# Attention scores of two heads in four contract over 68 partitions instead of 128, and two clears go

## The chip, the cores and the metric

The kernel runs on one core of a Trainium2 chip. The metric is the device time of one execution in microseconds, the median of the runs. The core's engines are PE (matrix multiply; PEld is its weight load), DVE (VectorE), ACT (ScalarE), POOL (GpSimd) and SP, which issues transfers. Each works through its own instructions in order and waits on semaphores for the others.

## What is computed

Eight batches of eight heads of causal attention over 576 positions with 64 features, with a bias from a running sum, and behind it a feed-forward block over all 4608 tokens:

```python
scores = q @ k.T / 8                       # per head, 576 x 576
cum    = cumsum(maximum(s, 0))
scores = where(causal, -1e9, scores + minimum(-(cum[i] - cum[j]), 0))
attn   = softmax(scores) @ v               # 64 heads
x      = attn, heads side by side          # 4608 x 512
g, val = x @ w_gate, x @ w_val             # 512 -> 1536
out    = (silu(g) * val) @ w_out           # 1536 -> 512
```

## The kernel before

The 64 heads are worked off in 16 half-batches of four heads. The query and key rows of a half-batch stand, transposed, in two tiles `KQ[i][0]` and `KQ[i][1]` (i is the half-batch modulo 2), each of 128 partitions, with an index for key side (0) and query side (1) and the positions of two heads, 2 x 576 columns, and 64 columns of padding behind them. In `KQ[i][0]` the 64 features are in partitions 0 to 63, in `KQ[i][1]` in partitions 64 to 127. The other 64 partitions carry the bias: four of them ("aug" rows: partitions 64 to 67 of the first tile, 0 to 3 of the second) hold the running sum, split into a high and a low bf16 part, against constant rows, so that one matmul gives the product of query and key and the bias in one sum. The remaining 60 are zero, so that the contraction over all 128 partitions is right. Heads 0 and 1 of a half-batch are in the first tile, heads 2 and 3 in the second.

`score_piece` (L352) makes the scores of one head, in four chunks of 512, 512, 512 and 64 columns, each in one PSUM bank; in all nine matmuls a head at L373, with 128, 128, 128, 128 / 448, 64 / 320, 192 / 64 columns. ACT takes the exponential (L383). For the first batch a mask matmul (L367) comes first in the chunks on the diagonal; for later batches POOL clears above the diagonal afterwards. `av_piece` (L410) multiplies with the values, DVE divides (L427). `gate_value` (L643) and the down projections (L700, L749) are the feed-forward block; they are mixed with the attention of later batches in an order that is written out by hand and by a list of costs, which fixes each engine's order of work.

The beginning is written out too. The clears of the 60 zero partitions stand there: DVE clears half of the columns of the first tile of half-batch 0 (L222), ACT both second tiles (L230), POOL the first tile of half-batch 1 (L234); `pads` (L226) clears the padding columns. DVE then makes the running sum (L240, L241), splits it into `HL` (L244 to L246) and copies transposed queries and keys out of PSUM (L330). For the very first head the aug rows are not brought by a transfer (`aug`, L188): PE picks them out of `HL` (L914), and ACT (L925) and DVE (L929) write all of partitions 64 to 127 of its columns. POOL issues the loads of half-batch 1 (L145) behind its clears, casts (L270), and issues the loads of v (L162).

Of the kernel before, what the change touches and what calls it, by code (L numbers as in the profile page):

```python
# [19 lines left out]
def kernel(  # L20
# [11 lines left out]
    nc = tc.nc  # L32
    PSUM = bass.MemoryType.PSUM

    B, H, S, D = q.shape
# [7 lines left out]
    NR = HB // 2  # L43
# [20 lines left out]
    def pt_col(tj, bi):  # L64
# [26 lines left out]
    KQ = [  # L91
        [const.tile([128, 2, NR * S + 64], BF16, name=f"kq{e}{i}") for e in range(2)]
        for i in range(2)
    ]
# [19 lines left out]
    with tc.manual_schedule():  # L114
# [10 lines left out]
        def take():  # L125
            b = min(bank, key=lambda x: released[x])
            assert released[b] < OPEN
            released[b] = OPEN
            return b

        def give(b):
            clock[0] += 1
            released[b] = clock[0]

        def view(b, w):
            return bank[b][:, 0:w]
# [42 lines left out]
        def aug_rows(i, r):  # L179
            r0 = 64 * (1 - r)  # L180
            return KQ[i][r][r0 : r0 + 64, :, :].bitcast(FP32)
# [37 lines left out]
        nc.vector.tensor_add(r_k[up], ident[up, 64:65], ident[up, 65:66])  # L219
        nc.vector.tensor_add(r_q[up], ident[up, 66:67], ident[up, 67:68])  # L220
        nc.vector.tensor_scalar_mul(r_m[up], r_q[up], -1.0)
        nc.vector.memset(aug_rows(0, 0)[:, :, S // 2 :], 0.0)  # L222

        def pads(i):
            for r in range(2):
                nc.gpsimd.memset(KQ[i][r][64 * r : 64 * r + 64, :, NR * S :], 0.0)  # L226

        for i in range(2):
            rows = aug_rows(i, 1)
# [1 line left out]
                rows.rearrange("p a n -> p (a n)"),  # L231
                one_s[0:64, 0:1].to_broadcast([64, NR * S + 64]), 0.0,
            )
        nc.gpsimd.memset(aug_rows(1, 0), 0.0)  # L234
        pads(0)
        pads(1)
        for nm in ("k", "q"):
            load_one(1, nm, eng=nc.gpsimd)
# [113 lines left out]
        def score_piece(bh, ci):  # L352
            hb, hh = divmod(bh, HB)
            masked = bh < H
            if ci == 0:
                pts[bh] = PTP[0].tile(
                    [128, PTW], BF16, tag="pt", bufs=PTP["bufs"], name="pt"
                )
            pt = pts[bh]
            r, e = divmod(hh, 2)  # L360
            T = KQ[hb % 2][r]
            bs = take()
            n = sum(hi - lo for _, lo, hi in CHUNKS[ci])
            sc = view(bs, n)
            masked_here = masked and ci in (0, 3)
            if masked_here:
                nc.tensor.matmul(  # L367
                    sc, ident, lower[:, 0:n], start=True, stop=False, skip_group_check=True
                )
            o = 0  # L370
            for (tj, lo, hi) in CHUNKS[ci]:
                w = hi - lo
                nc.tensor.matmul(  # L373
                    sc[:, o : o + w],
                    T[:, 1, e * S + 128 * tj : e * S + 128 * (tj + 1)],
                    T[:, 0, e * S + lo : e * S + hi],
                    start=not masked_here,
                    stop=True,
                    skip_group_check=masked_here,
                )  # L380
                o += w
            c0 = CHUNK_PT[ci]
            nc.scalar.activation(pt[:, c0 : c0 + n], sc, AF.Exp, scale=0.125)  # L383
            give(bs)
            if masked:
                return
            if ci == 0:
                nc.gpsimd.affine_select(  # L388
                    pt[:, 1088:1600], pt[:, 1088:1600], pattern=[[0, 4], [1, 128]],
                    compare_op=ALU.is_ge, fill=zreg, base=0, channel_multiplier=-1,  # L390
                )
            if ci == 3:
                nc.gpsimd.affine_select(
                    pt[:, 512:576], pt[:, 512:576], pattern=[[1, 64]],
                    compare_op=ALU.is_ge, fill=zreg, base=0, channel_multiplier=-1,
                )
# [164 lines left out]
        def attn_items():  # L561
            for kk in range(H, BH + 2):
                h, step = divmod(kk, HB)
                if kk < BH:
                    if step == 0:
                        do_later(NR * 2)
                    if step == 1 and 3 < h + 1 < NPE:
                        cast_one(h + 1, "k", nc.gpsimd)
                        cast_one(h + 1, "q", nc.gpsimd)
                    if step == 2 and 3 < h + 1 < NPE:  # L570
                        aug(h + 1, GP4)
                    for ci in range(4):
                        score_piece(kk, ci)
                        side(h, step, ci)
                        side_v(h, step, ci)
                        yield kk + 0.1 + ci / 8
                        if (step, ci) in PREP_AT.get(h, ()):
                            prep_one(
                                h + 1, PREP_AT[h][step, ci],
                                (nc.scalar, nc.vector)[ci // 2] if h == 2 else None,  # L580
                            )
                            yield kk + 0.1 + ci / 8
# [357 lines left out]
        def scores(h):  # L940
            for ci in range(4):
                score_piece(h, ci)
# [22 lines left out]
        picked_row(0)  # L965
        row_half("k", 1)
        score_piece(0, 0)
        score_piece(0, 1)
        row_half("q", 1)
# [151 lines left out]
```

## Time and profile before

| | |
|---|---|
| median of 3 runs | 374.26 us (373.94 to 375.38) |
| the profiled execution's own time | 373.92 us |
| its span, first to last instruction | 372.0 us |
| mean granted clock of PE | 0.998 |
| PE busy | 363.2 us |
| score matmuls L373, 576 in all: mean with 128 / 64 / 448 / 320 / 192 columns | 219 / 193 / 352 / 299 / 246 ns |
| their weight loads, mean | 98 ns |
| DVE clear L222, POOL clear L234 | 0.59 us, 1.11 us |

A matmul's row has the active rows and columns of the array ahead of its shape: 128\*128 is all of it, 64\*128 are 64 partitions contracted. Matmuls are pipelined, so the duration of one is a latency that overlaps the next; the throughput is the distance between starts. A time such as "8.44 0.89" is the start and the length in microseconds.

### The profile page before, as it was taken

Reading aid. Unit: us, or ns where it says so; the run is one execution under the profiler, and the core shown is the slowest. Engines: PE = TensorE matmul, PEld = TensorE weight load, DVE = VectorE, ACT = ScalarE, POOL = GpSimd, SP = SyncE. Lnnn points to the kernel's source line nnn. Section 1 sums busy time; section 2 is a strip of 40 time slices with the busy share of each in tenths; the row PEclk is TensorE's granted clock in tenths of the full one; section 3 lists DMA queues with packets and bytes.
Section 4 is the critical chain, followed back from the end, with each engine's and each line's share of the span. In section 5 each row is a group of like instructions: output and inputs, shape, how many; then the busy total and the mean of one; then the engine's idle time right before and its main releaser. Section 6 shows DMA issues by size and latency. Waiting matters only on the chain.

```text
span 372.0 us, 8786 instructions
## 1 busy us (share of the span) xinstructions
PE 363.2 (98%) x3288; PEld 230.3 (62%) x3288; DVE 291.1 (78%) x585; ACT 239.9 (65%) x470; POOL 212.4 (57%) x325
## 2 busy tenths in 40 slices
PE   7899999999999999999999999999999999999996
PEld 6684556655555557855685558655865585476465
DVE  8978776377985899589967897699868867975984
ACT  8877776778886967688757875786565523323321
POOL 8983556955266547594749464955675516315320
PEclk9999999999999999999999999999999999999999
DMA  7999999799879996996789484994142113002003
GB/s 238 220 254 259 215 272 257 239 299 227 252 172 307 199 268 181 162 285 217 214 179 263 160 185 157 265 210 114 40 121 62 35 30 118 0 3 86 28 0 113
DMA packets 97133, 64.21 MB, mean 173 GB/s; under 512 B 77228, under 2 KB 82724, under 8 KB 97092
## 3 DMA queue, kind: packets, MB, share of 16 engines
q1 hardware_dynamic: 84964, 41.46, 46.9%
q0 software_dynamic: 12128, 22.21, 22.7%
q8 instruction: 25, 0.41, 0.5%
q14 instruction: 16, 0.13, 0.1%
HBM read 37.90 MB, written 19.86 MB: 155 GB/s over the span
## 4 chain that ended last, share of the span: by engine, by line
PE 83%; DVE 10%; DMA 2%; ACT 2%; issue 2%; POOL 1%; DVEq 0%; ACTq 0%
PE banks L643 43%; PE banks L749 17%; PE banks L373 9%; PE banks L410 7%; PE banks L700 5%; DVE kq L330 3%; DMA pk<-ks 2%; DVE pp L666 2%; DVE ht L677 1%; DVE kq L288 1%; ACT th L664 1%; POOL vt L173 1%; ACT pt L383 1%; PE banks L459 1%; PE banks L301 0%
## 5 line engine op out<-in xcount | busy, mean ns | idle before, releaser
L383 ACT ACTIVATE pt<-banks 128x512 bf16<-128x512 f32 (+1 forms) x256 | 120.4, 511 | 29.8 <-PE banks L373 17.1
L643 PE MATMUL banks<-XT,wg 128*128 128x512 bf16 x432 | 111.4, 379 | 0.4 <-DVE pp L666 0.3
L643 PE MATMUL banks<-XT,wv 128*128 128x512 bf16 x432 | 110.9, 379 | 0.1
L664 ACT ACTIVATE th<-banks 128x512 bf16<-128x512 f32 x108 | 64.7, 599 | 56.3 <-PE banks L643 51.4
L666 DVE SCALAR_TENSOR_TENSOR pp<-th,banks 128x512 bf16<-128x512 bf16 x108 | 73.7, 682 | 18.3 <-ACT th L664 18.0
L677 DVE SCALAR_TENSOR_TENSOR ht<-pp,banks 128x512 bf16<-128x512 bf16 x108 | 74.1, 687 | 10.3
L373 PE MATMUL banks<-kq 128*128 128x128 bf16 (+4 forms) x576 | 76.4, 240 | 0.8 <-DVE kq L330 0.3
L686 POOL TENSOR_TENSOR ht<-ht 128x512 bf16<-128x512 bf16 x35 | 40.4, 1154 | 53.3 <-DVE su L684 53.2
L373 PEld LDWEIGHTS <-kq 128*128 128x128 bf16 x576 | 46.1, 98 | 30.7 <-issue 2.4
L643 PEld LDWEIGHTS <-wv 128*128 128x128 bf16 x432 | 38.4, 98 | 36.2 <-issue 0.2
L643 PEld LDWEIGHTS <-wg 128*128 128x128 bf16 x432 | 38.4, 98 | 34.1 <-issue 0.7
L410 PEld LDWEIGHTS <-pt 128*128 128x128 bf16 x960 | 41.8, 98 | 17.7 <-issue 0.7
L388 POOL TENSOR_SCALAR_AFFINE_SELECT pt<-pt 128x512 bf16<-128x512 bf16 x56 | 36.6, 653 | 25.9 <-ACT pt L383 21.7
L410 PE MATMUL banks<-vt,pt 128*128 128x65 bf16 x960 | 46.8, 194 | 0.5 <-DVE ot L427 0.4
L444 POOL DMA_DIRECT2D xs<-ot x24 | 21.7, 904 | 30.4 <-DVE ot L427 28.0
L749 PEld LDWEIGHTS <-ht 128*128 128x128 bf16 x336 | 31.2, 98 | 4.3
L427 DVE TENSOR_TENSOR ot<-banks,rc 128x320 bf16<-128x320 f32 x64 | 31.5, 492 | 2.2
L188 POOL DMA_DIRECT2D kq<-HL x48 | 29.2, 610 | 0.0
L700 PE MATMUL banks<-wo,ht 128*128 128x512 bf16 x96 | 25.8, 379 | 0.0
L749 PEld LDWEIGHTS <-su 128*128 128x128 bf16 x252 | 23.6, 98 | 3.3
L814 POOL TENSOR_TENSOR ysb<-ysb 128x512 f32<-128x512 f32 x12 | 15.2, 1269 | 15.3 <-DVE ysb L808 15.3
L749 PE MATMUL banks<-WS,ht 128*128 128x256 bf16 x168 | 22.9, 273 | 0.0
(101 smaller groups left out, 377.2 us busy)
## 6 DMA issues: line engine op xcount, KB each, us to landing
out_dram<-ysb POOLq DMA_DIRECT2D x32, 256.0 KB, 4.0
rawv<-in_v_dram SPq DMA_DIRECT2D x28, 256.0 KB
rawk<-in_k_dram SPq DMA_DIRECT2D x12, 576.0 KB
rawq<-in_q_dram SPq DMA_DIRECT2D x12, 576.0 KB
xs<-ot POOLq DMA_DIRECT2D x24, 160.0 KB, 3.7
ks<-ck SPq DMA_DIRECT2D x11, 288.0 KB
qs<-cq SPq DMA_DIRECT2D x11, 288.0 KB
rawk<-in_k_dram POOLq DMA_DIRECT2D x3, 576.0 KB, 6.0
```

Of the source, the lines that this page charges most:

```text
L373: nc.tensor.matmul(sc[:, o : o + w], T[:, 1, e * S + 128 * tj : e * S + 128 * (tj + 1)], T[:, 0, e * S + lo : e * S + hi], start=not maske ...
L383: nc.scalar.activation(pt[:, c0 : c0 + n], sc, AF.Exp, scale=0.125)
L388: nc.gpsimd.affine_select(pt[:, 1088:1600], pt[:, 1088:1600], pattern=[[0, 4], [1, 128]], compare_op=ALU.is_ge, fill=zreg, base=0, channel ...
L410: nc.tensor.matmul(av[:, bi * (D + 1) : (bi + 1) * (D + 1)], pt[:, c0 : c0 + 128], VT[b % 2][:, tj, h, :], start=(tj == 0), stop=(tj == bi),)
L427: nc.vector.tensor_mul(ot[:, :, e * D : (e + 1) * D], av3[:, :, 0:D], rc[:, :, None].to_broadcast([128, NCH, D]),)
L643: nc.tensor.matmul(view(bs, TT), w[:, c, f0 : f0 + 128], xt[:, c, :], start=(c == 0), stop=(c == 3),)
L664: nc.scalar.activation(th, pg, AF.Tanh, scale=0.5)
L666: nc.vector.scalar_tensor_tensor(pp, in0=th, scalar=1.0, in1=pg, op0=ALU.add, op1=ALU.mult)
L677: nc.vector.scalar_tensor_tensor(hp[:, 2 * k2 : 2 * k2 + 2, :].rearrange("p a n -> p (a n)"), in0=pp, scalar=0.5, in1=pv, op0=ALU.mult, op ...
L686: (nc.vector if ft == NFT - 1 else nc.gpsimd).tensor_sub(hp[:, 1:3, :], hp[:, 1:4:2, :], hp[:, 0:3:2, :])
L700: nc.tensor.matmul(view(pys[ts_], DM), hps[ft // 2][:, 2 * (ft % 2) + half, c0 : c0 + 128], WO[j][:, ft % WKO, :], start=(ft == 0), stop=( ...
L749: nc.tensor.matmul(ps, lhs(p), rhs(p), start=(first and p == 0), stop=(last and p == NP - 1), skip_group_check=True,)
```

## The change

The scores of heads 0 and 1 of each half-batch take only partitions 0 to 67 of the first tile, the features and the four aug rows; those of heads 2 and 3 still take all 128. The two clears of zero partitions of the first tiles go, and `pads` clears the padding of the query side alone, for the first tile over all partitions. The order of everything else is as it was.

```diff
-        nc.vector.memset(aug_rows(0, 0)[:, :, S // 2 :], 0.0)
 
         def pads(i):
             for r in range(2):
-                nc.gpsimd.memset(KQ[i][r][64 * r : 64 * r + 64, :, NR * S :], 0.0)
+                nc.gpsimd.memset(KQ[i][r][64 * r :, 1, NR * S :], 0.0)
...
-        nc.gpsimd.memset(aug_rows(1, 0), 0.0)
         pads(0)
         pads(1)
...
             r, e = divmod(hh, 2)
-            T = KQ[hb % 2][r]
+            T = KQ[hb % 2][r][0 : 68 if r == 0 else 128]
             bs = take()
```

## The prediction, made before the changed kernel was built or run

> **What bounds the kernel now.** I read the page first, then the busy time by stretches, the chain of waits of the first 20 us, the timeline of the same stretch, and one line's own view. The page's span and its row of busy time:
>
> ```profile
> span 372.0 us, 8786 instructions
> ...
> PE 363.2 (98%) x3288; PEld 230.3 (62%) x3288; DVE 291.1 (78%) x585; ACT 239.9 (65%) x470; POOL 212.4 (57%) x325
> ```
>
> The busy time by stretches says where the missing 2% lie (stretch, its length, then each engine's busy time):
>
> ```profile
> 0.00:9.30 9.30, 7.05 (x68) 5.58 (x69) 7.93 (x19) 7.74 (x10) 8.28 (x19) 1.00 0.72 238
> 9.30:19.00 9.70, 8.38 (x96) 6.05 (x96) 9.54 (x15) 8.47 (x21) 9.58 (x14) 1.00 1.01 219
> 19.00:100.00 81.00, 79.81 (x840) 48.95 (x836) 59.41 (x116) 63.78 (x125) 47.93 (x81) 1.00 1.05 253
> 100.00:200.00 100.00, 99.60 (x935) 63.50 (x932) 79.92 (x166) 72.86 (x145) 62.97 (x99) 1.00 0.92 219
> 200.00:300.00 100.00, 100.00 (x928) 63.55 (x926) 82.61 (x173) 66.85 (x135) 61.96 (x93) 1.00 0.57 139
> ```
>
> From 19 us on PE hardly ever idles. "Busy" overlaps, so I also took the distance from each matmul's start to the next in the trace and subtracted its columns at 2.4 per ns: from 19 us to the last matmul at 368 us all of that comes to 11.6 us, mostly 2 to 3 ns on each of some 3100 matmuls; real stalls are about 3 us. So after 19 us the time is the number of columns that PE streams, and only two things can move it: the price of a score matmul, and when the dense part begins. What sets that beginning is in the chain of waits (start, length, what):
>
> ```profile
> 3.11 0.59 DVE kq L222
> 3.70 0.03 issue
> 3.73 0.56 DVE s_sb L240
> ...
> 6.97 0.80 DVE HL L246
> 7.77 0.61 DVE kq L330
> 8.38 0.06 issue
> 8.44 0.17 DVE kq L929
> ```
>
> The clear at L222 stands in a DVE line without gaps: prefix sum, split into HL, first copies, row L929. From 9.24 to 19.36 DVE goes on so, 9.54 busy of 9.70 us. The timeline shows who else meets it:
>
> ```profile
> 2.61 1.11 POOL L234 MEMSET kq<- 64x1216 f32 x1
> ...
> 4.85 0.91 POOL L145 DMA_DIRECT2D rawk<-in_k_dram  x1
> ...
> 6.15 0.69 PE L315 MATMUL banks<-ident,cq 128*64 128x128 bf16 x9
> ...
> 6.77 1.15 PE L914 MATMUL banks<-HL,sel 64*128 64x512 bf16 x8
> ...
> 7.86 0.69 PE L315 MATMUL banks<-ident,ck 128*64 128x128 bf16 x9
> 8.00 0.82 ACT L925 ACTIVATE kq<-banks,r_m,r_k 64x576 bf16<-64x576 f32 x1
> ...
> 8.44 0.89 DVE L929 TENSOR_SCALAR kq<-banks,r_q,r_k 64x576 bf16<-64x576 f32 x1
> ...
> 8.87 0.38 PE L367 MATMUL banks<-lower,ident 128*128 128x512 bf16 x1 [0.33 <-ACT kq L925]
> ```
>
> The first score matmul starts at 9.38, when L929 (8.44 + 0.89 = 9.33) is done; the ACT row that it also needs was done at 8.82.
>
> **The change, part by part.** *The DVE clear.* One instruction, 0.59 us and 0.03 of issue: 0.62 us off the line, if the s values (its next step, L240) have landed by 3.11. They were issued first, at 0.81, and L240 followed the clear without a wait, so they landed before 3.73; between 2.1 and 4.0 us the queues moved 0.47 MB, three times their 0.14 MB. I take all 0.62; the bound below is 0. How far does it carry? L246 then ends at 7.15, the copy L330 runs 7.18 to 7.89, and L929 becomes ready at 7.92. But its input is the pick L914, whose last matmul ends at 6.77 + 1.15 = 7.92, plus some 0.06: 7.98. That is the stall's new owner: the pick follows the transposes of q, these follow ACT's cast, this a load, and none of them is touched. So L929 moves from 8.44 to 7.98, by 0.46 us, and 0.16 is lost. ACT's row (8.82) and PE's mask matmul (8.87) now come last before the first score, which starts near 9.09 in place of 9.38; but what carries on is DVE, its copies and the cast L260 0.46 earlier each. They need the second half of the transposes (last one done near 8.55, copy at 8.78) and the load of half-batch 1, next. **-0.46 us.**
>
> *The POOL clear.* 1.11 us at 2.61, followed by the pads and then by what POOL issues: the two loads of half-batch 1 at 4.85 and 5.75, two casts, five loads of v. No instruction is moved past another. The loads can be issued 1.16 us earlier, at 3.69. Their data came 2.3 us after the issue, with the rate row of 4 to 8 us (0.1 us each) low before:
>
> ```profile
> GB/s 415 369 369 392 415 392 415 415 392 369 415 369 369 392 369 415 415 323 461 461 277 138 115 92 207 138 92 184 92 46 46 46 323 230 507 230 323 415 323 507
> ```
>
> The first half-batch's own loads end at 6.0 and the next data start at 7.2; shifted by 1.16 they start at 6.0, in that hole, so they take nothing from the loads before. The casts L270 (6.54) then wait for data rather than POOL; their users on PE (7.86 and 9.91) stand behind the pick and the scores. The v loads start some 0.5 us earlier. All of it lies beside DVE's line: 0, while L260 gets its data by 10.27 (it had them by 10.73, and they come about 1.1 earlier). Uncovered, it would cost at most those 0.46 us.
>
> *The pads.* Four memsets as before, half the columns, two of them over twice the partitions: 198 to 418 ns each before, at most the same after, on POOL beside DVE: 0 (at best another 0.5 us for POOL, which nothing reads).
>
> *The matmuls.* 288 of the 576 at L373 and their weight loads have 68 active rows for 128. No row shows 68. The nearest are the picks, with 64 rows: starts of the first and the last lie 1.15 - 0.19 (mean of the 64-column form) = 0.96 us apart, seven slots, four of 512 columns at 0.216 (PE's 0.86 us for four in the chain) and three of 64: (0.96 - 0.86)/3 = 0.03 us each. With 128 rows the values at L410 give (1.07 - 0.19)/29 = 0.03 us for 65 columns. So 64 rows stream and load weights as fast as 128, no faster: **0 us**, and no gain from fewer rows either. The weight load itself takes 94 ns there and 98 in L373, hidden behind the matmul before.
>
> Sum: 0.62 - 0.16 = 0.46 us, against the profiled execution's own 373.92 us (1.9 us around its span): 373.46. The median of the runs lies 0.34 above that execution, so 373.8 us. The matmuls decide the sign, so two rules are weighed there. The Trainium skill, TensorEngine Tiling (Array Packing), Key Properties, says that changing the tiling mode drains the array, and it lists row tilings of 128, 64 and 32 rows only. By it 68 rows stay in the 128-row mode and nothing drains; by the same page's drains for every change the sum would be that of the first rival. The same skill's main page, Trainium Kernel Development and Optimization, Best Practices, says always to tile to 128 partitions: it speaks against the change without a price, and the pick's slots above speak against it.
>
> **The rivals.** *Slower: changing the number of active rows drains PE.* Place: every border between these matmuls and others. The rows around the pick show a price: the nine transposes end their slots at 6.15 + 0.47 + 0.06 = 6.68, the pick starts at 6.77, 0.09 late; behind it L315 starts at 7.86 for an expected 7.76, 0.10 late. There rows or columns change between 128 and 64. In the trace's order the 288 matmuls have 190 borders: 190 x 0.095 = 18 us, 391.8 us. For it: each change of shape in the trace costs this, and no row tells "another number of rows" from "another mode". Against it: 68 is more than half the array, and all the rows that pay go to a half. It decides from 2.3/190 = 12 ns a border (0.5%, or 1.87 us, plus the 0.46).
>
> *Slower: 68 rows load weights slowly.* A load of 64 columns shows a slow form: the first matmul behind one waits 243 - 219 = 24 ns.
>
> ```profile
> L315 PE MATMUL banks<-ident,cq x18: 219/219/243, 6.2 to 10.4; 128*64 128x128 bf16 x18
> ```
>
> At that rate 128 columns take 48. Of the 288, 35 follow a matmul of 64 or 65 columns (slot 0.03): 35 x 20 ns = 0.7 us; 102 follow one of 128 columns, whose 55 ns just cover 48. Exposed each time, 288 x 48 = 13.8 us. So 374.5 to 387.6; it decides from 8 ns a score. I lean to the low end, as every load in the trace runs behind the matmul before; and the pick's 64-row loads fit into slots of 0.03 us. The Trainium skill, TensorE: Matmul & The Clock Gate, LDWEIGHTS, would give columns/1.2, 107 ns; by it an estimate of 8 us more.
>
> *Faster by more.* POOL's 1.16 us and the earlier data might shorten the stretch to 19 us beyond DVE's line (full 0.62, plus waits of PE, 0.7 and 0.3 us, on copies of L330), and remove the 1.3 us of waits left on PE afterwards: up to 2.5 us, 371.8. Against it: DVE is gapless there, and its remaining work is unchanged.
>
> **How the numbers follow.** 0.5% (1.87 us: below 372.4, above 376.1) is about what a measurement can tell here from no change. Forecast, 0 to 0.75 us gained and the runs' spread about it: 0.58, 373.2 to 374.8. Drain: 0.14. Slow loads: 0.18, of it 0.05 within 0.5% and 0.13 above. Faster by more: 0.10, of it 0.09 beyond 0.5%. Together: faster 0.09, same 0.58 + 0.05 + 0.01 = 0.64, slower 0.14 + 0.13 = 0.27. The range from 371.9 to 378.0 leaves out the drain, 0.05 of the slow loads and 0.01 below.
>
> **What would show it.** The matmuls of L373 half as 68*128 with the same 219, 193 and 352 ns; slots of 55 ns between their starts and no gap at their borders; L929 at about 7.98, first score near 9.1, the dense part 0.46 earlier, PE's busy total the same. Wrong: gaps of tens of ns before or behind rows of 68*128, a longer distance between their starts, L240 waiting for its load, or a cast L270 or L260 that waits for data.

## The result: 1.6 us slower, nearly all of it lost before the dense part begins

| | before | after |
|---|---|---|
| median of 22 runs each | 374.04 us (373.23 to 378.62) | 376.44 us (375.39 to 378.09) |
| profiled execution, its span | 373.92 us, 372.0 us | 375.92 us, 373.8 us |

The ratio on record is 1.0043, with a 95% interval from 1.0027 to 1.0059: about 1.6 us more, and a ratio of 1 lies outside it. The runs of each kernel scatter over several us, and other measures give more: the medians differ by 2.4 us, the lowest of 22 runs by 2.2 us. The forecast was 373.8 us and a small gain.

The changed file has two lines fewer from the clear on, so L240 of before is L238 of after, L260 is L258, L301 is L299, L373 is L371, L914 is L912 and L929 is L927.

The page of after, span and busy times:

```profile
span 373.8 us, 8743 instructions
...
PE 362.4 (97%) x3248; PEld 231.2 (62%) x3288; DVE 291.5 (78%) x584; ACT 240.0 (64%) x470; POOL 210.9 (56%) x324
```

PE's busy time did not grow (363.2 before). So look for a late start, not for slower matmuls. The values' matmuls mark the dense part; one line of each kernel, before and then after:

```profile
L410 PE MATMUL banks<-vt,pt x960: 190/193/198, 18.9 to 299.2; 128*128 128x65 bf16 x192
```

```profile
L408 PE MATMUL banks<-vt,pt x960: 190/193/198, 20.5 to 301.1; 128*128 128x65 bf16 x192
```

The first of 960 starts 1.6 us later and the last 1.9 us later; from first to last it takes 280.3 and 280.6 us. All but 0.3 us of the loss was there when the first of them began. Busy time by stretches of after names the stretch (its length, then PE, PEld, DVE, ACT, POOL, then the granted clock of PE):

```profile
9.30:19.00 9.70, 7.89 (x76) 5.96 (x76) 9.16 (x13) 6.51 (x15) 9.58 (x15) 0.82 0.82 169
```

PE works off 76 matmuls there in place of 96 and for part of it at half clock, and ACT falls from 8.47 to 6.51 us; POOL is as full as before, 9.58 us.

**POOL's queue is late.** The timeline of POOL in after (start, length, instruction, in brackets the wait ahead of it):

```profile
2.49 0.79 POOL L225 MEMSET kq<- 128x64 bf16 x4
3.23 0.91 POOL L145 DMA_DIRECT2D rawk<-in_k_dram  x1
...
6.82 0.75 POOL L268 CAST ck<-rawk 128x576 bf16<-128x576 f32 x1 [1.95 <-DMA rawk<-in_k_dram]
8.69 0.67 POOL L268 CAST cq<-rawq 128x576 bf16<-128x576 f32 x1 [1.12 <-DMA rawq<-in_q_dram]
...
13.71 1.16 POOL L258 CAST cq<-rawq 128x1152 bf16<-128x1152 f32 x1
```

The same casts before:

```profile
7.41 0.89 POOL L270 CAST cq<-rawq 128x576 bf16<-128x576 f32 x1
...
12.65 1.16 POOL L260 CAST cq<-rawq 128x1152 bf16<-128x1152 f32 x1
```

Read it in this order. The loads of half-batch 1 are issued at 3.23 instead of 4.85. The second-half casts of half-batch 0 now wait for their own data, 1.95 and 1.12 us, where before they waited for none; the query cast starts 1.28 us later. Everything behind it in POOL's queue is late: the five issues of v, and behind them the cast of half-batch 1's queries, by 1.06 us. The reading to be tested is that the earlier loads of the next half-batch delay the loads of the current one.

**Who reads that last cast.** PE transposes its result. PE in after, then the same step before:

```profile
9.48 0.60 PE L371 MATMUL banks<-kq 68*128 68x128 bf16 x6 [0.42 <-DVE kq L927]
...
13.46 0.44 PE L299 MATMUL banks<-ident,ck 128*128 128x128 bf16 x5 [1.43 <-DVE kq L328]
...
15.10 1.15 PE L299 MATMUL banks<-ident,cq 128*128 128x128 bf16 x9
```

```profile
13.93 0.67 PE L301 MATMUL banks<-ident,cq 128*128 128x128 bf16 x9
```

Before, the cast ended at 12.65 + 1.16 = 13.81 and the transposes of queries began at 13.93: a slack of 0.12 us. After, it ends at 13.71 + 1.16 = 14.87, so they cannot begin before that; they begin at 15.10, and at half clock (nine take 1.15 us instead of 0.67). Half clock lasts from 14.86 to 18.27 us in the trace's clock records, after PE had idled 1.43 us for keys that DVE copied late. In this one execution PE did not wait for POOL: the keys had made it late first, and POOL's cast had ended 0.23 us before. So both delays stand here side by side, and which of them belongs to the change is for the experiments to say.

**DVE has a second delay in this execution.** Its timeline of after:

```profile
3.83 0.56 DVE L238 TENSOR_SCALAR s_sb<-s_sb 64x576 f32<-64x576 f32 x1 [0.81 <-DMA s_sb<-in_s_dram]
...
8.54 0.89 DVE L927 TENSOR_SCALAR kq<-banks,r_q,r_k 64x576 bf16<-64x576 f32 x1
...
10.84 1.71 DVE L258 CAST ck<-rawk 128x1152 bf16<-128x1152 f32 x1
```

The same cast before:

```profile
10.73 0.76 DVE L260 CAST ck<-rawk 128x1152 bf16<-128x1152 f32 x1
```

The s values land only now: DVE idles 0.81 us where the clear stood, and L927 starts at 8.54 (8.44 before). And the cast of half-batch 1's keys takes 1.71 us instead of 0.76. The Trainium skill, SBUF — State Buffer, section "SBUF: two separate sides", says that DVE's two-port operations and GpSimd share a port pair that one of them holds for a whole instruction while the other stands still, and that transfers issued by GpSimd need it too. The runs below fit this but do not show it: beside POOL's issues of v this cast took 0.76 us before and in e11, 1.71 us in the change and 1.70 us in e14, and with these issues moved to SP it took 0.76 us in e5 and 1.47 us in e8, where POOL's own cast of the queries ran beside it.

**The matmuls behave as forecast.** Groups of after by shape (count, busy us, mean ns):

```profile
L371 PE MATMUL banks<-kq 128*128 128x128 bf16 x128 | 12.6, 222 | 0.0
L371 PE MATMUL banks<-kq 68*128 68x128 bf16 x128 | 12.4, 218 | 0.7 <-DVE kq L927 0.4 <-DVE kq L286 0.3
```

68 rows take 218 ns, 128 rows 222, and 219 before. Taken from the trace for the 172 of the 190 borders that lie behind 21 us, the mean distance between weight loads going from other work into these matmuls is 184.3 ns after and 184.8 before, and going out 125.3 and 125.1: no drain at the borders. Their weight loads take 97 ns.

### The profile page after: what moved, and what is told of

Its sections match the earlier page's. It is cut to its first block, busy times and chain, and to the rows that moved or that the text cites. A ratio compares the mean times of both kernels' runs of the same rounds, so it can differ in the third digit from the quotient of the medians.

```text
span 373.8 us, 8743 instructions
## 1 busy us (share of the span) xinstructions
PE 362.4 (97%) x3248; PEld 231.2 (62%) x3288; DVE 291.5 (78%) x584; ACT 240.0 (64%) x470; POOL 210.9 (56%) x324
## 4 chain that ended last, share of the span: by engine, by line
PE 85%; DVE 8%; DMA 3%; ACT 2%; issue 2%; DVEq 0%; ACTq 0%
PE banks L641 43%; PE banks L747 17%; PE banks L371 10%; PE banks L408 7%; PE banks L698 5%; DMA pk<-ks 2%; DVE kq L328 2%; DVE pp L664 2%; DVE ht L675 1%; PE banks L299 1%; DVE kq L286 1%; DMA s_sb<-in_s_dram 1%; ACT pt L381 1%; PE banks L457 1%; DVE ck L258 0%
## 5 line engine op out<-in xcount | busy, mean ns | idle before, releaser
L641 PE MATMUL banks<-XT,wv 128*128 128x512 bf16 x412 | 109.3, 379 | 1.1
L371 PE MATMUL banks<-kq 68*128 68x128 bf16 (+9 forms) x576 | 77.1, 242 | 1.2 <-DVE kq L927 0.4
L371 PEld LDWEIGHTS <-kq 68*128 68x128 bf16 (+1 forms) x576 | 46.5, 99 | 30.3 <-issue 2.4
L698 PE MATMUL banks<-wo,ht 128*128 128x512 bf16 x90 | 24.8, 379 | 0.3
L391 POOL TENSOR_SCALAR_AFFINE_SELECT pt<-pt 128x64 bf16<-128x64 bf16 x56 | 15.1, 270 | 15.0 <-ACT pt L381 14.9
```

Of the source, the lines that this page charges most:

```text
L371: nc.tensor.matmul(sc[:, o : o + w], T[:, 1, e * S + 128 * tj : e * S + 128 * (tj + 1)], T[:, 0, e * S + lo : e * S + hi], start=not maske ...
L641: nc.tensor.matmul(view(bs, TT), w[:, c, f0 : f0 + 128], xt[:, c, :], start=(c == 0), stop=(c == 3),)
L698: nc.tensor.matmul(view(pys[ts_], DM), hps[ft // 2][:, 2 * (ft % 2) + half, c0 : c0 + 128], WO[j][:, ft % WKO, :], start=(ft == 0), stop=( ...
```

## The experiments

The theory that the two traces suggest: the loss comes from the order of transfers and casts in the first 20 us, set off by POOL's loads starting early. The rivals: the 68-row matmuls themselves; the way that the transfers are issued (which queue); and the TensorE clock, which the longer idle time would leave at half. Kernels measured together share the runs of the kernel before. Executions of one kernel scatter by several us, those of the kernel before from 373.23 to 379.05, so the lowest run is read beside the ratio. "V" is a kernel made from the changed one, "B" one made from the kernel before.

| run | loads of half-batch 1 issued | second-half query cast starts | half-batch 1's query cast ends | lowest us | ratio (95%) |
|---|---|---|---|---|---|
| before | 4.85 | 7.41 | 13.81 | 373.23 | 1 |
| the change | 3.23 | 8.69 | 14.87 | 375.39 | 1.0043 (1.0027 to 1.0059) |
| e1, B: 68 rows only | 4.86 | 7.91 | 15.50 | 373.65 | 1.0016 (0.9984 to 1.0049) |
| e2, V: POOL clear back | 4.72 | 7.90 | 14.28 | 373.88 | 1.0033 (0.9996 to 1.0070) |
| e3, V: DVE clear back | 4.67 | 7.84 | 13.83 | 373.72 | 1.0030 (0.9996 to 1.0064) |
| e4, V: these loads on SP | 3.48, on SP | 8.69 | 15.06 | 375.91 | 1.0054 (1.0028 to 1.0080) |
| e5, V: v loads on SP | 3.24 | 8.60 | 12.27 | 379.56 | 1.0178 (1.0125 to 1.0232) |
| e6, B: 17 idle matmuls | 4.85 | 7.41 | 14.06 | 373.74 | 1.0013 (0.9977 to 1.0050) |
| e7, V: 17 idle matmuls | 3.23 | 8.72 | 14.89 | 374.87 | 1.0012 (0.9982 to 1.0042) |
| e8, V: e5 and e7 | 3.23 | 8.81 | 11.82 | 381.05 | 1.0197 (1.0142 to 1.0251) |
| e9, V: init_vt first | 5.38 | 7.89 | 14.32 | 373.69 | 1.0018 (0.9982 to 1.0054) |
| e10, V: e9 and 13 idle matmuls | 5.25 | 7.73 | 14.11 | 373.72 | 0.9990 (0.9963 to 1.0018) |
| e11, V: the change again | 3.23 | 9.37 | 15.68 | 374.97 | 1.0039 (1.0010 to 1.0068) |
| e12, B: 13 idle matmuls | 4.85 | 7.41 | 13.81 | 373.34 | 0.9988 (0.9955 to 1.0020) |
| e13, B: loads first | 2.51 | 9.96 | 16.11 | 375.64 | 1.0044 (1.0019 to 1.0070) |
| e14, V: loads 0.67 us later | 3.90 | 7.21 | 13.91 | 373.49 | 0.9981 (0.9954 to 1.0009) |
| e15, V: e14 and 13 idle matmuls | 3.90 | 7.32 | 13.86 | 373.54 | 1.0000 (0.9976 to 1.0025) |
| e16, V: e14 again | 3.90 | 7.78 | 13.95 | 373.63 | 1.0011 (0.9985 to 1.0038) |

**The matmuls alone (e1).** Both clears and the pads of before are kept.

```diff
-            T = KQ[hb % 2][r]
+            T = KQ[hb % 2][r][0 : 68 if r == 0 else 128]
```

> The kernel before with the 68-row slice alone; both clears and the old pads stay. Startup theory (the lost time comes from POOL issuing half-batch 1's loads 1.6 us earlier, not from the matmuls): the same as before, ratio 0.998 to 1.002, POOL's first load at 4.85, DVE's cast of half-batch 1's keys 0.76 us, no drop of PE's clock before 19 us. Matmul theory (68-row weights or their borders are dear): the same loss as the whole change, ratio about 1.004, spread over the span.

1.0016 with 1 inside, the lowest run 0.4 us above the lowest of before, and the values' matmuls take 280.0 us from first to last (280.3 before). No cost of 68 rows shows, and none of the gain that fewer rows might have brought. One sign missed its expectation: in the profiled execution, a long one of 377.34 us, the clock reached its full rate only at 9.44 us and fell to half again from 16.27 to 19.68, although the loads came at 4.86. Delays of that kind exist without early loads.

**One clear back (e2, e3).** To the changed kernel:

```diff
+        nc.gpsimd.memset(aug_rows(1, 0), 0.0)                       # e2, ahead of pads(0)
+        nc.vector.memset(aug_rows(0, 0)[:, :, S // 2 :], 0.0)       # e3, at its old place
```

> The change with POOL's clear of half-batch 1 put back, so that POOL's loads come about 1.1 us later again (near 4.3). Startup theory: ratio 0.998 to 1.002, casts of the second halves near 6.5 and 7.4, no wait of 1.4 us on PE at the transposes of half-batch 1. Matmul theory: ratio about 1.004. If the DVE clear is what matters: ratio about 1.004 too.

> The change with DVE's clear put back and POOL's left out. Startup theory: like the whole change, ratio 1.003 to 1.006, POOL's loads at 3.2, and DVE's L240 step at most 0.1 us later than in the whole change, because s lands at 3.8 anyway. If the missing DVE clear were the cause: ratio 1.000.

In e2 the loads start at 4.72, the second-half cast is back to 7.90, and the lowest run to 373.88; the median is not (375.89, against 375.09 for before beside it), the ratio missed the 0.998 to 1.002 of the startup theory, and the interval excludes neither 1 nor the change's 1.0043. e3 was meant to leave POOL early and missed: the pads waited 1.21 us for the DVE clear, which writes a neighbouring part of the same tile, so the loads came at 4.67; its lowest run is 373.72, its ratio 1.0030. Neither tells the clears apart by itself.

**Another queue (e4, e5).** e4 puts the early loads on SP. e5 leaves them on POOL but moves the five v loads to SP, so that POOL is free of issues while DVE casts.

```diff
-            load_one(1, nm, eng=nc.gpsimd)      # e4
+            load_one(1, nm)
...
+        load_v(0, range(5))                     # e5, on SP behind aug of half-batch 0
-        load_v(0, range(5), nc.gpsimd)
```

> The change with half-batch 1's two loads issued by SP, behind half-batch 0's, not by POOL. Startup theory (two queues share the transfer engines, so the early POOL loads slow the second halves): in one queue the second halves are no longer overtaken, casts L268 start near 6 and 7 us, POOL issues v's loads from about 7.7, no PE wait of 1.4 us: ratio 0.996 to 1.000. If the loads' earliness as such hurts, whatever the queue: ratio 1.003 or more. Matmul theory: ratio about 1.004.

> The change with the five loads of v issued by SP, behind the aug rows of half-batch 0, not by POOL. Theory A (the loss is POOL's line: its casts wait for data, the issues of v's loads come 1.05 us late and hold up DVE's cast of half-batch 1's keys and POOL's cast of its queries): DVE's cast back at 0.76 us, the cast of the queries by 12.5, no wait of 1.4 us on PE, ratio 0.996 to 1.000. Theory B (the second halves' late data alone are the loss): still 1.003 or more.

In e4, with the loads on SP, the second-half casts start at 8.02 and 8.69 (6.82 and 8.69 in the change), and the time is the change's: what was expected of two queues that share the engines failed, and what was expected if the loads' earliness hurts from any queue came true. The Trainium skill, DMA: Bandwidth & Descriptors, section "SWDGE vs HWDGE vs iDMA", says that each transfer engine takes turns between queues that software- and hardware-issued transfers feed separately; that would make POOL's queue the culprit, and e4 contradicts it as the only cause. Early loads hurt from either queue.

In e5 the casts came as expected (DVE's 0.76 us long, the queries' cast ended at 12.27), and the time was lost elsewhere. DVE's cast, then the wait that cost it (us in total, times, longest):

```profile
10.51 0.76 DVE L258 CAST ck<-rawk 128x1152 bf16<-128x1152 f32 x1
```

```profile
PE banks L371 <- DMA kq<-HL: 5.2, 1, 5.2
```

The cast's 0.76 us do not prove the reason, since it took as long beside POOL's issues before. PE reaches 15.92 us where before had the same matmul at 16.14, and then stands 5.2 us: the aug rows of half-batch 1 had been queued on SP behind v. So e5 cannot say what the v issues on POOL cost.

**The clock (e6, e7, e8, e12).** Idle matmuls into a bank that nobody reads keep PE busy: `fill(3)` and `fill(6)` behind the two halves' key rows, and eight more ahead of half-batch 1 in e6 to e8; in e12, four more of the warm-up at the start in place of those eight.

```diff
+        def fill(n):
+            for _ in range(n):
+                nc.tensor.matmul(banks[:, 0, 384:512], ident, ident, start=True, stop=True)
```

> The kernel before with 17 more matmuls on idle PE (3 behind the first transposes of keys, 6 behind their second half, 8 ahead of half-batch 1's), whose results nobody reads. It is the base for the next run. Theory C (most of the loss is PE's clock, which falls when PE idles): spread between runs smaller than before, lowest as before, ratio 0.996 to 1.000. Otherwise the 17 cost what they take, up to 0.9 us, ratio 1.000 to 1.003.

> The change with the same 17 matmuls. Theory C: as fast as the kernel before with them, ratio 0.998 to 1.002, no half clock between 9 and 19 us. Theory A: 0.003 above that run still, PE's clock full but DVE's cast 1.7 us and POOL's v loads late.

> The change with v's loads on SP and the 17 matmuls. Theory A: as the run with v's loads on SP alone. Theory C: as the change with the 17 matmuls. If both hold it is the fastest of the four, ratio 0.995 to 0.999.

> The kernel before with the same 13 matmuls. Theory C: median 0.5 us or more under the kernel before, spread below 2.5 us. Theory A adds that it is within 0.5 us of the run with the memsets moved and the 13 matmuls.

On the kernel before they gain nothing that shows: lowest runs of 373.74 and 373.34, intervals with 1 inside. On the changed kernel (e7) full clock holds from 6.93 us on, and the measures disagree: the lowest run falls by 0.5 us, from 375.39 to 374.87, which is still 1.1 us above e6's, as theory A has it, while the ratio, 1.0012 with 1 inside, lies where theory C put it; the medians of e7 and e6 are 375.56 and 375.01. So the clock's share is some half microsecond by the lowest runs and can be more by the ratio. It is not needed for the loss: the profiled executions of e4 and e13 (below) ran at full clock from 7.13 and 4.53 us to the last matmul, and took 376.65 and 375.64 us. e8 repeats e5's wait for the aug rows (3.9 us).

**The order on POOL put back by other means (e9, e10).** The clears of the value tiles (`init_vt`), which POOL has to do anyway, go ahead of the pads.

```diff
+        init_vt(0)          # ahead of pads(0); their old places go
+        init_vt(1)
```

> The change with POOL's four memsets on the tiles of values (0.32 and 0.52 us each, later needed anyway) moved from behind the loads to ahead of them: POOL's loads of half-batch 1 start at about 4.9, as in the kernel before, and no clear is done. Theory A (what hurts is that these loads come at 3.2): lowest run back from 375.4 to 373.9 or less, median ratio 0.996 to 1.001. If the missing clears hurt in another way, or the 68 rows do: lowest run stays above 375, ratio about 1.004.

> The same with 13 matmuls more in PE's early gaps (4 at the end of the warm-up, 3 and 6 behind the transposes of keys), to bring PE's full clock earlier whatever the phase. Theory C (the spread between runs is when PE's clock rises): spread below 2.5 us and median lower by 0.5 us or more than without them. Otherwise: as without them, or up to 0.7 us slower.

The loads come at 5.38 and 5.25, the second-half cast at 7.89 and 7.73, the lowest runs at 373.69 and 373.72. e10, with 13 idle matmuls, also scatters little, up to 375.59; e9 does not, up to 382.07, and its median is 376.04, so its ratio of 1.0018 missed the 1.001 foreseen. No gain over before is shown.

**The change itself once more (e11), for its trace.**

> The changed kernel itself, beside the others on one chip. Every theory: ratio 1.003 to 1.006, lowest run near 375.4.

1.0039, the change again. The POOL line and DVE of this execution:

```profile
9.37 0.67 POOL L268 CAST cq<-rawq 128x576 bf16<-128x576 f32 x1 [1.80 <-DMA rawq<-in_q_dram]
```

```profile
16.55 0.82 DVE L328 COPY kq<-banks 64x640 bf16<-64x640 bf16 x1 [1.96 <-PE banks L299]
```

Here DVE's cast was not held up (0.76 us), and yet the execution took 376.44 us: PE waited 1.53 us for POOL's cast, and DVE 1.96 us for PE. PE also ran at half clock from 15.51 to 18.92 us, so this execution alone does not show that POOL's late line is enough; e13's, at full clock, does.

**Early loads alone (e13) and the change without them (e14, e16).** What was still open was whether the start of the loads decides, with 68 rows and absent clears as bystanders. e13 is the kernel before, with 128 rows and both clears, its two POOL loads moved ahead of POOL's clear and pads. e14 is the change with one 0.52 us memset of the value tile moved ahead of the pads. e16 repeats it, and e15 adds the 13 idle matmuls.

```diff
-        nc.gpsimd.memset(aug_rows(1, 0), 0.0)     # e13: these three behind the two loads
-        pads(0)
-        pads(1)
...
+        nc.gpsimd.memset(VT[0][64:128, 4, :, 0:D], 0.0)     # e14: ahead of pads(0); its old place goes
```

> The kernel before, 128 rows and both clears kept, with one thing changed: POOL issues the two loads of half-batch 1 ahead of its clear and pads, at about 2.6 in place of 4.85. Theory A (early loads delay the first half-batch's second half, and with it POOL's whole line): lowest run 374.9 or more, ratio 1.003 to 1.008, POOL's cast of the second half's queries at 8.6 or later. If the 68 rows or the missing clears are needed for the loss: ratio 1.000, lowest run 373.3.

> The change with one memset of 0.52 us, needed later anyway, moved ahead of POOL's loads, which then start near 3.8, about where the prediction had put them. Theory A with a threshold where the two sets of loads meet: if 0.5 us are enough, lowest run 373.9 or less and ratio 0.998 to 1.002; if not, lowest run 374.5 or more and ratio 1.002 to 1.005.

> The change with the 0.52 us memset moved ahead of POOL's loads and the 13 matmuls in PE's early gaps. If the two repairs add (loads at 3.9, PE's full clock early): median under the kernel before by 0.5 us or more, ratio 0.995 to 0.998, spread under 2.5 us. If only the delay counts: ratio 0.998 to 1.001.

> The change with the 0.52 us memset moved ahead of the loads, once more, to see whether it beats the kernel before: ratio 0.996 to 1.000, lowest run 373.9 or less. Were the first measurement luck: ratio above 1.001.

POOL's timeline of e13 and the wait of PE for the last of POOL's casts, then POOL's timeline of e14:

```profile
2.51 0.91 POOL L145 DMA_DIRECT2D rawk<-in_k_dram  x1
...
9.96 0.67 POOL L270 CAST cq<-rawq 128x576 bf16<-128x576 f32 x1 [2.28 <-DMA rawq<-in_q_dram]
```

```profile
16.16 0.68 PE L301 MATMUL banks<-ident,cq 128*128 128x128 bf16 x9 [1.53 <-POOL cq L260]
```

```profile
3.90 0.91 POOL L145 DMA_DIRECT2D rawk<-in_k_dram  x1
...
7.21 0.88 POOL L270 CAST cq<-rawq 128x576 bf16<-128x576 f32 x1
```

e13 changes nothing but an order and costs 1.0044, as much as the change, with all 128 rows and both clears. e14 has everything of the change and no cost that shows: 0.9981 and, repeated, 1.0011, and neither interval reaches 1.0043. By its own expectation the 1.0011 says that e14's gain was luck. With the idle matmuls besides, e15 is at 1.0000: the two repairs do not add. So a start of the loads at 3.90 instead of 3.23 us is the difference between no loss that shows and 1.6 us. (e14 also takes the 0.52 us memset out of POOL's queue behind the queries' cast; that cannot have made this cast earlier, but its own small effect is not separated.)

The lowest runs of all kernels agree: with the loads issued at 3.48 us or earlier they are 374.87 or more (the change, e4, e7, e11, e13, and e5 and e8 with their own loss), with the loads at 3.90 or later 373.88 or less, in all eleven. The ratios are less sharp. Three kernels with late loads, e2, e3 and e9, have 1.0018 to 1.0033, so a smaller loss of another origin is not excluded for them.

The transfers themselves show the delay. In the trace's packets, SP's loads of s and of half-batch 0 are 576 packets of 2304 bytes. The last of them ends at 6.54 us before, at 8.17 in the change, 8.78 in e11 and 9.28 in e13, and at 6.76 and 7.07 in e14 and e16. In the six kernels whose POOL issued its loads at 3.24 us or earlier it ends between 8.01 and 9.28 us, in the eleven with 3.90 or later between 6.54 and 7.50 (e4 has both sets of loads on SP in packets of one size). Why POOL's loads stretch the last of SP's so much stays open: POOL's first packet started at 5.96 us in the change and at 6.03 in e14.

**How the delay becomes time.** In 16 of the 18 profiles (all but e5 and e8, which wait for the aug rows) I set the start of PE's nine transposes of half-batch 1's queries against that execution's own time: from 13.93 us and 373.92 us (before) over 14.07 and 373.71 (e16), 14.33 and 374.54 (e2), 15.10 and 375.92 (the change), 15.73 and 376.44 (e11) to 17.78 and 377.70 (e3). A straight line through all 16 has a slope of 1.0 and a correlation of 0.91, with a residue of 0.5 us. What is lost there is not given back. POOL's cast is a floor under that start: in nine of the 16 profiles PE began within 0.25 us of its end, before, the change, e4, e11 and e13 among them. In the change it ends at 14.87 at the earliest of its three profiles with unmoved v loads (the change, e7, e11), 1.06 us later than before, which would keep every execution about 1 us above the lowest times of before; the lowest runs of the change and e11 are 375.39 and 374.97. Above the floor each execution has its own delays: in e14's profile DVE's cast was held up (1.70 us), PE waited 1.41 us for its keys and ran at half clock from 13.85 to 17.27 us, its transposes began at 15.71 and the time was 375.86, though POOL was punctual. The profiles of e1, e3 and e6, where POOL's loads came at 4.67 us or later, have such delays too, with transposes at 17.15, 17.78 and 15.35 us.

## Why the prediction was wrong

1. *What bounds the kernel:* right. From 20 us on the two executions run alike within 0.3 us, and it was the start of the dense part that moved.
2. *The matmuls, 0:* right. The picks with 64 rows were the proper nearest row. The two slower rivals fell: 190 borders cost nothing that shows, and 68-row weights load in 97 ns behind the matmul before. So did "faster by more".
3. *The DVE clear, -0.46:* wrong by its condition. The sum took "all 0.62" between the bounds 0 and 0.62, arguing from the volume moved by 4 us. That does not say when one transfer lands. In the runs without the clear, L238 waited for s and began between 3.56 and 3.83 us, against 3.73 before. The clear had filled a wait for data; its removal bought 0.17 us at best and next to nothing on average, which is the lower bound. The other half was right: where DVE was a little earlier (e2, e4, e14, e16), L927 waited for the pick.
4. *The POOL clear, 0:* the step that failed. Three terms of it were off. First, "the loads can be issued 1.16 us earlier, at 3.69" came out as 3.23: the clear's 1.16 us, and 0.46 us more from pads that took 0.79 us for 1.12 and began 0.12 earlier. The prediction had priced that half microsecond in its next step as one "which nothing reads". Second, "in that hole, so they take nothing from the loads before" was misread and left no margin: data at 6.0 against loads that end at 6.0, taken from a row of rates. The packets of before have SP's loads ending at 6.54 us and POOL's first packet at 6.46, so there was no room of that size. At 3.90 (e14) the loads before were done by 6.76 all the same; at 3.23 only by 8.17. The 3.69 of the prediction was not run. Third, "all of it lies beside DVE's line: 0" looked at the keys' cast, which DVE does, and never at the queries' cast at the end of POOL's own queue. The profile of before had the answer: it ended at 13.81, and its reader began at 13.93. With 0.12 us of slack nearly all of a delay of POOL's line goes through to PE: it came to 1.06 us, where the prediction gave "at most those 0.46 us". So the sum that was to be -0.46 us had about 0 for the DVE clear and a loss, some 1 us of it POOL's floor, for the POOL clear.
5. *The list of what would make it wrong* named the sign that came true, casts and L240 waiting for data, but no rival with a price stood for it.

What stays open: how much of the 1.6 us is POOL's floor (about 1 us by the profiles), how much the clock (some 0.5 us by the lowest runs of e7, more by its ratio) and how much DVE's held-up cast, which comes and goes from one execution to the next.

No version that beats the kernel before was found; e14 equals it as far as two measurements tell (0.9981 and 1.0011), with two clears fewer.

## What to carry to other kernels

Removing idle-looking work at the head of a queue can cost time: here the clear was also a delay that kept the next stage's loads out of the way of the current stage's. When a change lets transfers start earlier, compare the new start with the end of the transfers in flight, with a margin for every instruction ahead of it, and follow the whole queue down to the last instruction that another engine reads, with its slack. A gap-free engine is not proof that its work bounds it: check when the data behind each removed instruction would land.

## What was not expected of the hardware

- 0.67 us in the issue of two loads (3.90 or 3.23 us) moved the landing of other, earlier-issued loads far enough that a cast that reads them began between 7.21 and 7.78 in the one case (e14 to e16) and at 8.69, 8.72 or 9.37 in the other (the change, e7, e11). With the early loads on the same queue as those others (e4) it was 8.69 too.
- The same DVE cast took between 0.76 us (before) and 2.10 us (e3) in different executions, and in two of the changed kernel 1.71 and 0.76 us.
- PE's clock first reached its full rate at 4.62 us in after's execution, at 5.31 in before's and at 17.42 in e3's. The half-clock stretch in after lasted 18.27 - 14.86 = 3.41 us, in e1 19.68 - 16.27 = 3.41 us. The Trainium skill, TensorE: Matmul & The Clock Gate, Part 1, describes a free-running window of 3413 ns; these two stretches agree.
